# A top-k attention followed by a mixture of experts: the last batch's scores are computed at the start and kept in DRAM

## Chip, cores, metric

One core of a Trainium2 chip. The metric is the device time of one execution in microseconds; lower is better. Three runs of the kernel before gave 1983.19, 1984.89 and 1987.19 us, median 1984.89.

## What is computed

```python
def _attn_ref(q, k, v):                    # (4 batches, 8 heads, 576 rows, 64)
    scores = scale * np.matmul(q, k.transpose(0, 1, 3, 2))
    kth = np.partition(scores, -32, axis=-1)[..., -32:-31]
    scores = np.where(scores >= kth, scores, -1e9)
    attn = softmax(scores)
    return attn @ v
def _moe_ref(x, w_gate, w1, w2):           # x: (2304, 512), 8 experts, hidden 1024
    P = exp(x @ w_gate - max);  P = 8 rounds of row and column normalisation
    for e in range(8):
        out += P[:, e:e+1] * (np.maximum(x @ w1[e], 0) @ w2[e])
```

The attention output, its heads side by side, is the x of the second part. All experts see all rows.

## The kernel before

**Numbers.** All is float32. TensorE is fed with pairs: a rounded high part made by ScalarE (`hi_act`, line 75) and the rest, made by a subtraction on GpSimd (`lo_pool`, L81) or on VectorE (`lo_dve`, L84). A product of two such operands is three matmuls, or two in the scores, where q holds its high part in partitions 0 to 63 and its low part in 64 to 127.

**Attention** runs in seven stages (`STAGES`, L25), in this order: batch 0 rows 0 to 255, batch 0 rows 256 to 511, the same two of batch 1, both of batch 2, the last 64 rows of batch 0 (`attend_rest`), and both of batch 3. Each stage walks four pairs of heads. For a pair `attend_heads` loads q, k and v, splits them, and `attend_phase` takes two tiles of 128 rows for each of the two heads: `scores` (L116, L117) makes a 128x576 tile in the one PSUM tile `sp`, with four matmuls of 288 columns; `copy_scores` (L125, L123) brings it to an SBUF tile `s` on ScalarE; `topk` runs four MAX8 and three MATCH_REPLACE8 on VectorE and masks the exponentials (`Et`, L145); `normalise` scales; TensorE transposes (L233), the result is split again and multiplied with v (L246, L247). The last 64 rows of two heads go through `rest_weights` as one more tile of scores (12 matmuls, 2304 columns).

**Experts.** Rows are grouped in blocks of 256. Blocks 0 to 4 take turns on two seats (`BOARD`, L32): block i boards at turn 4i and stays for 8 turns, one expert each (`visit`). A visit loads w1 and w2 (tile `wr`, L395), splits them (`wh` on ScalarE, `wl` on GpSimd), makes the hidden layer (L413, stored by L462 and L463) and the output (L500), which goes to DRAM through tile `y` (L508, L510). For block 0, half of the hidden layer (the first 256 of 512 inputs) is made early by `first_half` for all eight experts, 32 PSUM tiles of it: weights in `wr` (L432), matmuls L443, copy to `y` L446, store to DRAM L448. The first turns read it back with L452 and need only the other half. When attention has ended, `sinkhorn` makes P, `right_factors` (L563 and the lines around it) prepares blocks 5 to 8, which are then multiplied in a seven-product scheme (L611) with the output part L670, while the stored outputs are read back (L524) and summed.

**What sets the order.** The program is written as one stream; a planner orders it for each engine when the kernel is built, by priority (attention first, by `high_priority`), then by the place in the program, and each engine runs its list strictly in order. Tiles of one name share a fixed number of buffers: `wr` 3, `wh` and `wl` 6 each, `y` 4, PSUM `p2` 2, `p1` 2, `s` 3, `raw` 3, `kh` and `kl` 2 each. `first_half` and all visits use `wr` and `y`. All DMAs of the lines named here are issued from the SP queue.

Of the kernel before, what the change touches and what calls it, by code (L numbers as in the profile page):

```python
# [36 lines left out]
LAST = [5, 6, 7, 8]  # L37
OFF = {(0, 0): 3}
# [5 lines left out]
def kernel(  # L44
# [74 lines left out]

    def copy_scores(sp):  # L120
# [45 lines left out]
    def attend_heads(b, hp, phases, xts, xm):  # L166
# [13 lines left out]
        if phases:  # L180
            qs = load_phase(phases[0])
        ks = []
        for i in range(2):
# [18 lines left out]
        for ph in phases:  # L202
            if ph != phases[0]:
                qs = load_phase(ph)
            last = ph == phases[-1] and xm is not None
            qm = load_q("qm", 1024, 256, 1) if last else None
            attend_phase(hp, qs, qm, ks, xts[ph], xm if last else None, OFF.get((b, ph), 0))
# [3 lines left out]
    def attend_phase(hp, qs, qm, ks, xt, xm, off):  # L211
# [3 lines left out]
        for t in range(2):  # L215
# [3 lines left out]
            for i in range(2):  # L219
                o = i * 256 + t * 128  # L220
                qc = qs[:, o:o + 128]
                sp = scores([((a, 0, 288), [(qc, ks[i], slice(a * 288, a * 288 + 288))]) for a in range(2)])
                units.append((copy_scores(sp[:, :, 0:288]), Et[:, i, :], st[:, 0, i:i + 1]))
# [12 lines left out]
        if xm is not None:  # L236
            def put(rows, blocks, src):
                evac(ath[rows, blocks, 256:320], atl[rows, blocks, 256:320], src)
            rest_weights(qm, ks, put)
# [16 lines left out]
    def rest_weights(qm, ks, put):  # L256
        Et = ap_.tile([128, 2, S], F32, name="Et", bufs=2)
        st = ap_.tile([128, 2, 2], F32, name="st", bufs=3)
        qa, qb = qm[:, 0:128], qm[:, 128:256]
        sp = scores([  # L260
            ((0, 0, 256), [(qa, ks[0], slice(0, 256)), (qb, ks[1], slice(64, 320))]),
            ((0, 256, 512), [(qa, ks[0], slice(256, 512)), (qb, ks[1], slice(320, 576))]),
            ((1, 0, 64), [(qa, ks[0], slice(512, 576)), (qb, ks[1], slice(0, 64))]),
        ])
        topk([(copy_scores(sp.rearrange("p a b -> p (a b)")[:, 0:S]), Et[:, 0, :], st[:, 0, 0:1])])
# [12 lines left out]
    def attend_rest(b, hp, qm, ks, xm):  # L278
# [7 lines left out]
        rest_weights(qm, ks, put)  # L286
# [408 lines left out]
    x2 = psx = None  # L695
    stages_until(-1)
# [71 lines left out]
```

## Time and profile before

| | |
|---|---|
| median of 3 runs | 1984.89 us (1983.19 to 1987.19) |
| the profiled execution: time, span | 1985.03 us, 1982.8 us |
| mean granted TensorE clock | 0.987 of full |
| TensorE busy (matmul) | 1886.4 us, 95% |
| VectorE, GpSimd, ScalarE busy | 1478.0, 1100.1, 1045.3 us |
| DMA | 238.97 MB, mean 121 GB/s |

The time exceeds the span by 2.2 us of start and end. Matmuls overlap each other, so a matmul's duration is longer than what it costs TensorE; the distance from one start to the next is what it costs. Instructions of VectorE, ScalarE and GpSimd stand one behind the other, with an overlap of less than 0.15 us.

### The profile page before, as it was taken

Reading aid. Unit: us, or ns where it says so; the run is one execution under the profiler, and the core shown is the slowest. Engines: PE = TensorE matmul, PEld = TensorE weight load, DVE = VectorE, ACT = ScalarE, POOL = GpSimd, SP = SyncE. Lnnn points to the kernel's source line nnn. Section 1 sums busy time; section 2 is a strip of 40 time slices with the busy share of each in tenths; the row PEclk is TensorE's granted clock in tenths of the full one; section 3 lists DMA queues with packets and bytes.
Section 4 is the critical chain, followed back from the end, with each engine's and each line's share of the span. In section 5 each row is a group of like instructions: output and inputs, shape, how many; then the busy total and the mean of one; then the engine's idle time right before and its main releaser. Section 6 shows DMA issues by size and latency. Waiting matters only on the chain.

```text
span 1982.8 us, 27234 instructions
## 1 busy us (share of the span) xinstructions
PE 1886.4 (95%) x9571; PEld 1581.2 (80%) x9571; DVE 1478.0 (75%) x2828; ACT 1045.3 (53%) x1715; POOL 1100.1 (55%) x978
## 2 busy tenths in 40 slices
PE   4798889999999999999999999899999999999998
PEld 3677778988887888888888888778888888888887
DVE  9999999999998999962999996335555555543333
ACT  5766657666666666655665666443333333333331
POOL 4557876665564455455554457895454554545440
PEclk9899989999999999999999999999999999999999
DMA  3477554444343333234433325333333333311111
GB/s 114 129 241 240 179 189 143 153 136 140 122 128 121 108 111 122 90 127 139 132 122 100 103 94 176 123 121 122 101 101 111 116 105 109 102 55 57 56 42 43
DMA packets 95785, 238.97 MB, mean 121 GB/s; under 512 B 10784, under 2 KB 12960, under 8 KB 95648
## 3 DMA queue, kind: packets, MB, share of 16 engines
q1 hardware_dynamic: 95648, 237.23, 37.3%
q8 instruction: 75, 1.23, 0.3%
q14 instruction: 62, 0.51, 0.1%
HBM read 203.11 MB, written 34.08 MB: 120 GB/s over the span
## 4 chain that ended last, share of the span: by engine, by line
PE 55%; DVE 34%; POOL 3%; DMA 3%; issue 2%; ACT 2%; SPq 0%; POOLq 0%; ACTq 0%; DVEq 0%
PE p L670 18%; DVE m L136 11%; DVE w L143 9%; PE p L611 9%; PE p L500 8%; PE p L413 8%; DVE Et L145 5%; PE pc L611 4%; DVE hl L463 4%; DVE atl L84 3%; PE pb L611 2%; POOL wl L81 2%; DMA wr<-in_w_dram 1%; PE pt L233 1%; DMA raw<-in_q_dram 1%
## 5 line engine op out<-in xcount | busy, mean ns | idle before, releaser
L81 POOL TENSOR_TENSOR wl<-wr,wh 128x1024 fp32r<-128x1024 f32 x280 | 683.1, 2451 | 466.3 <-ACT wh L75 453.1
L75 ACT ACTIVATE wh<-wr 128x1024 fp32r<-128x1024 f32 x280 | 294.6, 1059 | 270.2 <-PE p L611 181.6
L136 DVE MAX8 m<-w 128x8 f32<-128x576 f32 x432 | 317.8, 748 | 1.7
L413 PE MATMUL p<-xh,wh 128*128 128x256 f32 (+1 forms) x768 | 266.6, 347 | 13.1 <-DVE y L458 7.3
L413 PE MATMUL p<-xh,wl 128*128 128x256 f32 (+1 forms) x768 | 264.3, 345 | 0.2 <-POOL wl L81 0.2
L413 PE MATMUL p<-xl,wh 128*128 128x256 f32 (+1 forms) x768 | 263.8, 344 | 0.0
L500 PE MATMUL p<-wh,hl 128*128 128x512 f32 x640 | 248.0, 398 | 4.5 <-DVE hl L463 4.5
L500 PE MATMUL p<-wh,hh 128*128 128x512 f32 x640 | 252.0, 397 | 0.3 <-ACT hh L462 0.3
L500 PE MATMUL p<-wl,hh 128*128 128x512 f32 x640 | 250.8, 395 | 0.2 <-POOL wl L81 0.2
L517 DVE SCALAR_TENSOR_TENSOR acc<-p,P,acc 128x512 f32<-128x512 f32 x120 | 89.5, 750 | 167.3 <-PE p L670 167.3
L143 DVE MATCH_REPLACE8 w<-m,w 128x576 f32<-128x576 f32 x288 | 213.2, 741 | 0.2
L670 PE MATMUL p<-wh,h2h 128*128 128x512 f32 x512 | 199.8, 391 | 1.3 <-ACT h2h L634 0.7
L670 PE MATMUL p<-wl,h2h 128*128 128x512 f32 x512 | 199.9, 390 | 0.0
L670 PE MATMUL p<-wh,h2l 128*128 128x512 f32 x512 | 196.7, 390 | 0.0
L413 PEld LDWEIGHTS p<-xh,wh 128*128 128x128 f32 x768 | 148.7, 194 | 34.1 <-DVE y L458 9.6
L145 DVE SCALAR_TENSOR_TENSOR Et<-s,m,Et 128x576 f32<-128x576 f32 x144 | 161.4, 1128 | 16.8 <-ACT Et L139 15.8
L413 PEld LDWEIGHTS p<-xh,wl 128*128 128x128 f32 x768 | 149.0, 194 | 14.6 <-issue 0.4
L413 PEld LDWEIGHTS p<-xl,wh 128*128 128x128 f32 x768 | 149.0, 194 | 14.5
L500 PEld LDWEIGHTS p<-wh,hl 128*128 128x128 f32 x640 | 120.4, 189 | 28.6 <-DVE hl L463 6.2
L500 PEld LDWEIGHTS p<-wl,hh 128*128 128x128 f32 x640 | 120.9, 189 | 23.6 <-POOL wl L81 0.6
L500 PEld LDWEIGHTS p<-wh,hh 128*128 128x128 f32 x640 | 121.0, 190 | 23.0 <-issue 1.3
L152 ACT ACTIVATE Et<-Et,st 128x576 f32<-128x576 f32 x144 | 104.9, 770 | 55.8 <-DVE st L150 55.6
(179 smaller groups left out, 4059.8 us busy)
## 6 DMA issues: line engine op xcount, KB each, us to landing
wr<-in_w_dram SPq DMA_DIRECT2D x240, 512.0 KB, 3.5
y<-y SPq DMA_DIRECT2D x160, 256.0 KB, 2.7
raw<-in_k_dram SPq DMA_DIRECT2D x56, 288.0 KB, 3.0
wr<-in_w_dram SPq DMA_DIRECT2D x48, 256.0 KB, 3.6
raw<-in_q_dram SPq DMA_DIRECT2D x32, 256.0 KB, 3.0
p<-y SPq DMA_DIRECT2D x32, 256.0 KB, 3.5
y<-p SPq DMA_DIRECT2D x32, 256.0 KB, 4.1
raw<-in_v_dram SPq DMA_DIRECT2D x28, 288.0 KB, 3.0
```

The source lines that it names most:

```text
L75: nc.scalar.activation(dst, src, AF.Copy)
L81: nc.gpsimd.tensor_tensor(dst, src, hi.bitcast(F32), op=OP.subtract)
L136: nc.vector.max(m8[u][:, r, :], ws[u] if r else s)
L143: nc.vector.match_replace(ws[u], m8[u][:, r, :], ws[u] if r else s, LOWEST)
L145: nc.vector.scalar_tensor_tensor(Em, s, m8[u][:, 3, 7:8], Em, op0=OP.is_ge, op1=OP.mult, accum_out=rsum)
L152: nc.scalar.activation(Et[:, i, :], Et[:, i, :], AF.Copy, scale=st[:, 1, i:i + 1])
L413: nc.tensor.matmul(ps[:, fo, :], a[:, kk, fs], x[:, k0 + kk, cs], start=(i == 0), stop=(i == 3 * nk - 1))
L463: nc.vector.scalar_tensor_tensor(seat.hl[:, ft, cs], src, 0.0, seat.hh[:, ft, cs].bitcast(F32), op0=OP.max, op1=OP.subtract)
L500: nc.tensor.matmul(ps, a[:, ft, ts], m[:, ft % 2, :], start=(i == 0), stop=(i == 3 * NFT - 1))
L517: return nc.vector.scalar_tensor_tensor(ACC[t], y, g, ACC[t], op0=OP.mult, op1=OP.add)
L611: nc.tensor.matmul(ps, w[:, kk, :], x[:, kk, :], start=(fresh and i == 0), stop=(i == 5), skip_group_check=True)
L670: nc.tensor.matmul(ps, a[:, ft, ts], m[:, ft, :], start=(i == 0), stop=(i == 11))
```

## The change

The scores of batch 3 are made by a new generator, `scores_ahead`. It is stepped eight times, ahead of everything else in the program and at ordinary priority (below attention, and ahead of `first_half` and the visits). A step takes one head: it loads and splits k and q in the tiles `wr`, `wh` and `wl`, and for each of four tiles of 128 rows makes the scores in two halves of 288 columns, in PSUM tile `p2`; each half is copied by ScalarE to a tile `y` and stored to DRAM. Every second step adds the tile of the last 64 rows. When batch 3 is attended, `load_scores` brings each tile from DRAM to an `s` buffer (for the second head: to a buffer of `kh` or `kl`), in place of loading and splitting q and k, of the matmuls and of the copy. The core of the diff:

```diff
+AHEAD = [3]
...
+    def keep(key, parts):
+        kept[key] = dram.tile([128, S], F32, name="s" + "_".join(map(str, key)))
+        c = 0
+        for groups in parts:
+            ps = ps2.tile([128, 512], F32, name="p2")
+            y = op_.tile([128, 512], F32, name="y", bufs=YB)
+            n = 0
+            for width, terms in groups:
+                for i, (qc, (kh, kl), cs) in enumerate(terms):
+                    nc.tensor.matmul(ps[:, n:n + width], qc, kh[:, cs], start=(i == 0), stop=False)
+                    nc.tensor.matmul(ps[:, n:n + width], qc, kl[:, cs], start=False, stop=(i == len(terms) - 1))
+                n += width
+            nc.scalar.activation(y[:, 0:n], ps[:, 0:n], AF.Copy)
+            nc.sync.dma_start(kept[key][:, c:c + n], y[:, 0:n])
+            c += n
+
+    def load_scores(*key):
+        name = "s" if key[-1] == 0 or len(key) == 2 else ("kh", "kl")[key[3]]
+        s = ap_.tile([128, S], F32, name=name, bufs=NS if name == "s" else 2)
+        nc.sync.dma_start(s, kept[key])
+        return s
+
+    def scores_ahead():
+        for b in AHEAD:
+            for hp in range(HP):
+                ks, qm = [], None
+                for i in range(2):
+                    kr = wp.tile([128, S], F32, name="wr", bufs=WR)
+                    nc.sync.dma_start(kr, k[b, 2 * hp + i])
+                    kh = wp.tile([128, S], F32R, name="wh", bufs=WB)
+                    kl = wp.tile([128, S], F32R, name="wl", bufs=WB)
+                    hi_act(kh, kr)
+                    lo_pool(kl, kr, kh)
+                    ks.append((kh, kl))
+                    m = 512 + (256 if i == 0 else 0)
+                    qr = wp.tile([128, m], F32, name="wr", bufs=WR)
+                    for ph in range(2):
+                        o = ph * 512 + i * 256
+                        nc.sync.dma_start(qr[:, ph * 256:ph * 256 + 256], q[b, hp, :, o:o + 256])
+                    if i == 0:
+                        nc.sync.dma_start(qr[:, 512:768], q[b, hp, :, 1024:1280])
+                    qs = wp.tile([128, m], F32R, name="wh", bufs=WB)
+                    hi_act(qs, qr)
+                    lo_pool(qs[64:128], qr[64:128], qs[64:128])
+                    if i == 0:
+                        qm = qs[:, 512:768]
+                    for ph in range(2):
+                        for t in range(2):
+                            qc = qs[:, ph * 256 + t * 128:ph * 256 + t * 128 + 128]
+                            keep((b, hp, ph, t, i), [[(288, [(qc, ks[i], slice(a * 288, a * 288 + 288))])]
+                                                     for a in range(2)])
+                    if i == 1:
+                        groups = [(d[2] - d[1], terms) for d, terms in rest_groups(qm[:, 0:128], qm[:, 128:256], ks)]
+                        keep((b, hp), [groups[0:2], groups[2:3]])
+                    yield
+
+    early = scores_ahead()
...
-        for i in range(2):
+        for i in range(0 if ahead else 2):
             kr = ap_.tile([128, S], F32, name="raw", bufs=RAW)
...
+                if b in AHEAD:
+                    s = load_scores(b, hp, ph, t, i)
+                else:
+                    o = i * 256 + t * 128
+                    qc = qs[:, o:o + 128]
+                    s = copy_scores(scores([((a, 0, 288), [(qc, ks[i], slice(a * 288, a * 288 + 288))])
+                                            for a in range(2)])[:, :, 0:288])
...
+        if b in AHEAD:
+            s = load_scores(b, hp)
+        else:
+            sp = scores(rest_groups(qm[:, 0:128], qm[:, 128:256], ks))
...
     x2 = psx = None
+    for _ in range(8):
+        next(early, None)
     stages_until(-1)
```

## Rows read from the trace of the kernel before

**Rows 1.** The page: busy time of each engine, and the span in 40 equal slices (a digit is TensorE's busy share in tenths).
```profile
PE 1886.4 (95%) x9571; PEld 1581.2 (80%) x9571; DVE 1478.0 (75%) x2828; ACT 1045.3 (53%) x1715; POOL 1100.1 (55%) x978
...
PE   4798889999999999999999999899999999999998
```

**Rows 2.** Busy time by stretch: start and end of the stretch, its length, then busy us (and instructions) of PE, PE's weight loads, DVE, ACT, POOL, then granted clock, DMA share, GB/s.
```profile
0.00:77.00 77.00, 35.78 (x144) 27.73 (x145) 72.31 (x153) 47.80 (x81) 40.38 (x68) 0.89 0.30 89
77.00:156.00 79.00, 75.53 (x394) 63.66 (x393) 72.89 (x157) 57.25 (x109) 39.00 (x55) 1.00 0.76 247
156.00:295.00 139.00, 114.17 (x648) 98.36 (x648) 137.61 (x233) 88.39 (x139) 107.73 (x91) 0.93 0.60 198
295.00:935.00 640.00, 631.00 (x3502) 538.11 (x3501) 572.60 (x1192) 403.83 (x691) 355.72 (x347) 1.00 0.39 126
935.00:1242.00 307.00, 303.73 (x1658) 259.64 (x1656) 285.50 (x590) 193.97 (x330) 166.88 (x156) 1.00 0.37 121
1242.00:1318.00 76.00, 67.35 (x376) 56.99 (x374) 23.92 (x77) 35.29 (x53) 70.43 (x49) 0.93 0.38 122
1318.00:1983.00 665.00, 658.80 (x2860) 536.66 (x2860) 313.15 (x430) 218.73 (x315) 319.97 (x215) 1.00 0.28 87
```

**Rows 3.** Groups of PE instructions, shapes apart, in the stretch of batch 3's attention (935 to 1242 us): count, then busy us and mean ns of one, then idle time before them. L117 has as many as L116 of each shape.
```profile
L116 PE MATMUL sp<-kh,qs 128*128 128x288 f32 x64 | 19.2, 309 | 0.0
...
L116 PE MATMUL sp<-kh,qm 128*128 128x256 f32 x16 | 4.2, 292 | 0.0
...
L116 PE MATMUL sp<-kh,qm 128*128 128x64 f32 x8 | 1.7, 235 | 0.0
```

**Rows 4.** PE's instructions in order of time: start us, duration us. Two pairs that follow each other without a break, one of 288 and one of 256 columns.
```profile
1185.62 0.29 PE L116 MATMUL sp<-kh,qs 128*128 128x288 f32 x1
1185.75 0.30 PE L117 MATMUL sp<-kl,qs 128*128 128x288 f32 x1
...
1199.52 0.28 PE L117 MATMUL sp<-kl,qm 128*128 128x256 f32 x1
1199.64 0.28 PE L116 MATMUL sp<-kh,qm 128*128 128x256 f32 x1
```

**Rows 5.** Single lines of the program: duration in ns as min/median/max, then the first and the last start in us; for a DMA the last row of each is the time from issue to landing. `first_half`'s copy and store, and the load that reads it back.
```profile
L446 ACT ACTIVATE y<-p x32: 572/592/620, 78.4 to 156.5; 128x512 f32<-128x512 f32 x32
...
L448 SPq DMA_DIRECT2D p<-y x32: 326/327/2362, 79.0 to 157.7; - x32
...
DMA to landing us min/median/max: 2.0/3.5/6.7
...
L452 SPq DMA_DIRECT2D y<-p x32: 319/380/1342, 155.7 to 449.2; - x32
```

**Rows 6.** Groups of ACT instructions in the whole span, shapes apart (columns as in Rows 3).
```profile
L75 ACT ACTIVATE kh<-raw 128x576 fp32r<-128x576 f32 x56 | 36.9, 680 | 13.3 <-PE sp L116 10.5 <-DMA raw<-in_k_dram 2.5
L75 ACT ACTIVATE qs<-raw 128x512 fp32r<-128x512 f32 x32 | 20.1, 629 | 27.4 <-DMA raw<-in_q_dram 27.4
L446 ACT ACTIVATE y<-p 128x512 f32<-128x512 f32 x32 | 18.9, 592 | 5.3 <-PE p L443 4.9 <-ACT lg L333 0.4
L160 ACT ACTIVATE tl<-pt 128x384 f32<-128x384 f32 x24 | 11.7, 485 | 4.5 <-POOL atl L81 2.7 <-PE pt L233 1.7
```

**Rows 7.** Groups of POOL instructions in the whole span.
```profile
L81 POOL TENSOR_TENSOR kl<-raw,kh 128x576 fp32r<-128x576 f32 x54 | 81.6, 1521 | 36.1 <-ACT kh L75 32.0 <-PE pt L233 3.9
L81 POOL TENSOR_TENSOR qs<-raw,qs 64x512 fp32r<-64x512 f32 x31 | 41.3, 1331 | 28.6 <-ACT qs L75 20.8 <-issue 3.5 <-PE pt L247 2.4
```

**Rows 8.** The masking instruction `Et` on VectorE from 0 to 100 us, and in the whole span (columns as in Rows 5).
```profile
L145 DVE SCALAR_TENSOR_TENSOR Et<-s,m,Et x14: 796/804/1511, 17.2 to 94.2; 128x576 f32<-128x576 f32 x14
...
L145 DVE SCALAR_TENSOR_TENSOR Et<-s,m,Et x144: 791/812/3017, 17.2 to 1222.5; 128x576 f32<-128x576 f32 x144
```

**Rows 9.** VectorE's instructions in order of time, between batch 0's last rows and batch 3: start us, duration, and in brackets the idle time before it and what ended it.
```profile
901.91 0.82 DVE L145 SCALAR_TENSOR_TENSOR Et<-s,m,Et 128x576 f32<-128x576 f32 x1 [15.43 <-ACT Et L139]
...
928.92 0.76 DVE L136 MAX8 m<-s 128x8 f32<-128x576 f32 x1 [5.99 <-ACT s L123]
```

**Rows 10.** Single lines again (columns as in Rows 5): the store of a visit's output and the load that brings it back at the end of the kernel.
```profile
L510 SPq DMA_DIRECT2D y<-y x80: 319/327/432, 187.1 to 1313.5; - x80
...
L524 SPq DMA_DIRECT2D y<-y x80: 319/320/694, 1312.5 to 1729.4; - x80
```

**Rows 11.** The chain that ended last, in the stretch 130 to 150 us: start us, us, what.
```profile
132.23 1.73 PE p L443 x8
```

**Rows 12.** Groups of PE instructions from 156 to 295 us (columns as in Rows 3): those of attention. L117 has as many as L116, L247 as many as L246.
```profile
L246 PE MATMUL pt<-ath,vz 128*128 128x256 f32 x40 | 10.3, 287 | 1.1 <-DVE atl L84 1.1
...
L233 PE MATMUL pt<-idt,Et 128*128 128x128 f32 x57 | 9.5, 290 | 1.2 <-DVE atl L84 0.7 <-ACT Et L152 0.5
L116 PE MATMUL sp<-kh,qs 128*128 128x288 f32 x28 | 9.3, 346 | 12.3 <-ACT s L125 12.3
```

**Rows 13.** SP's own waits from 0 to 160 us: who waited for whom, us in total, times, longest.
```profile
SPq L448 <- ACT y L446: 28.5, 19, 2.8
```

**Rows 14.** The chain that ended last, in the stretch 1195 to 1335 us: between the end of attention and the last part.
```profile
1244.65 1.82 PE pt L325 x8
...
1261.59 2.64 POOL tf L563 x3
...
1317.96 1.19 PE pc L611 x4
```

More of the change, by code (lines that the diff above doesn't have):

```diff
@@ L118, in scores, with rest_groups @@
         return sp
+    def rest_groups(qa, qb, ks):
+        return [
+            ((0, 0, 256), [(qa, ks[0], slice(0, 256)), (qb, ks[1], slice(64, 320))]),
+            ((0, 256, 512), [(qa, ks[0], slice(256, 512)), (qb, ks[1], slice(320, 576))]),
+            ((1, 0, 64), [(qa, ks[0], slice(512, 576)), (qb, ks[1], slice(0, 64))]),
+        ]
+    kept = {}
+    def keep(key, parts):
[13 more added lines that the diff above has]
+            c += n
@@ L178, in load_phase @@
             return load_q("qs", ph * 512, 512, 2)
-        if phases:
-            qs = load_phase(phases[0])
+        ahead = b in AHEAD
+        qs = load_phase(phases[0]) if phases and not ahead else None
         ks = []
-        for i in range(2):
+        for i in range(0 if ahead else 2):
             kr = ap_.tile([128, S], F32, name="raw", bufs=RAW)
@@ L202, in attend_heads, with attend_phase @@
         for ph in phases:
-            if ph != phases[0]:
+            if ph != phases[0] and not ahead:
                 qs = load_phase(ph)
             last = ph == phases[-1] and xm is not None
-            qm = load_q("qm", 1024, 256, 1) if last else None
-            attend_phase(hp, qs, qm, ks, xts[ph], xm if last else None, OFF.get((b, ph), 0))
+            qm = load_q("qm", 1024, 256, 1) if last and not ahead else None
+            attend_phase(b, hp, ph, qs, qm, ks, xts[ph], xm if last else None, OFF.get((b, ph), 0))
         if not phases:
             attend_rest(b, hp, load_q("qm", 1024, 256, 1), ks, xm)
-    def attend_phase(hp, qs, qm, ks, xt, xm, off):
+    def attend_phase(b, hp, ph, qs, qm, ks, xt, xm, off):
         nq = 256 if xm is None else 320
@@ L219, in attend_phase @@
             for i in range(2):
[L220 to L223, printed above, removed]
+                if b in AHEAD:
[5 more added lines that the diff above has]
+                                            for a in range(2)])[:, :, 0:288])
+                units.append((s, Et[:, i, :], st[:, 0, i:i + 1]))
             topk(units)
@@ L238, in put @@
                 evac(ath[rows, blocks, 256:320], atl[rows, blocks, 256:320], src)
-            rest_weights(qm, ks, put)
+            rest_weights(b, hp, qm, ks, put)
         tmp = ap_.tile([128, 320], F32, name="tmp", bufs=1)
@@ L252, in attend_phase, with rest_weights @@
                 nc.vector.tensor_tensor(xm[r, hp, :], av[r, 256:320], tmp[r, 256:320], op=OP.add)
-    def rest_weights(qm, ks, put):
+    def rest_weights(b, hp, qm, ks, put):
         Et = ap_.tile([128, 2, S], F32, name="Et", bufs=2)
         st = ap_.tile([128, 2, 2], F32, name="st", bufs=3)
[L259 to L265, printed above, removed]
+        if b in AHEAD:
+            s = load_scores(b, hp)
+        else:
+            sp = scores(rest_groups(qm[:, 0:128], qm[:, 128:256], ks))
+            s = copy_scores(sp.rearrange("p a b -> p (a b)")[:, 0:S])
+        topk([(s, Et[:, 0, :], st[:, 0, 0:1])])
         normalise(Et, st, 1)
@@ L284, in put @@
             nc.scalar.activation(at[rows, blocks, :], src, AF.Copy)
-        rest_weights(qm, ks, put)
+        rest_weights(b, hp, qm, ks, put)
         av = pst.tile([128, 512], F32, name="pt")
```

## The prediction

> **What bounds the kernel now.** I read the page first: TensorE is busy 95% of the span, and in the 40 slices it falls short only in the first ones [rows 1]. Then I cut the span by stages [rows 2]. From 295 us to the end PE is short of full by 9.0, 3.3, 8.7 and 6.2 us in stretches of 640, 307, 76 and 665 us: it is the bound there. Before that it is short by 41.2 us up to 77 us, by 3.5 us up to 156 us, and by 24.8 us up to 295 us. VectorE is nearly full to 295 us as well, with attention; it is the bound of the first 77 us, where PE has nothing but attention's matmuls.
>
> So matmuls taken out of the stretch behind 295 us shorten the kernel one for one, as long as what they cost at the start is free. That is the whole question.
>
> **What is removed behind 295 us.** Batch 3's scores are 64 matmuls of 288 columns on L116 and as many on L117, 16 and 16 of 256, and 8 and 8 of 64 [rows 3]. Their mean durations (309 ns) can't be added, since matmuls overlap; from start to start it is 0.13 us for 288 columns and 0.12 us for 256 [rows 4]. That makes 128 x 0.13 + 32 x 0.12 + 16 x 0.12 at most = 22.3 us. The ends are 20.5 us (the short ones free) and 25 us (0.1 us more for some 25 of the changes between scores and other work). I take 23 us. The 36 copies on ScalarE, the splitting of k and q on GpSimd and ScalarE, and 20 loads also leave this stage; PE is full beside them, so I count nothing. VectorE keeps all its work, 285.5 of 307 us in that stage [rows 2]. The 36 loads that come in are 288 KB each and can run ahead by the buffers of `s`, `kh` and `kl`; against some 8 us of VectorE for a tile (307 us for 36) stand 3.5 us from issue to landing, as for the 256 KB stores of `first_half` [rows 5], so they are covered. If the cover failed, VectorE would wait and PE would go on with visits.
>
> **What the same work costs at the start.** On PE 23 us, against 41.2 us of idle time up to 77 us: it fits. The engine that is short is ScalarE. For each of the eight heads it has one split of k (680 ns for 576 columns), one of q (629 ns for 512; with the 256 columns of the last rows about 840 ns), and eight copies of 288 columns. No row has that size; 384 columns took 485 and 512 took 592 ns [rows 6], so about 405 ns. Four last-row tiles add 592 and about 220 ns each. The sum of durations is 64 x 0.405 + 8 x 0.68 + 4 x 0.63 + 4 x 0.84 + 4 x 0.59 + 4 x 0.22 = 40.5 us; with 0.1 us of overlap for each of the 88 it is 32 us. These are the two ends. Attention leaves ScalarE 77 - 47.8 = 29.2 us up to 77 us, of which some 5 us come before the first k and q can have landed: 24 us. From 77 to 156 us it is busy 57.25 us, 18.9 us of it the copies of `first_half`, so 38.4 us are attention's and 0.51 us of each us is free [rows 2, 6]. The early scores end at 77 + (32 - 24)/0.51 = 93 us, or at 77 + (40.5 - 24)/0.51 = 109 us. I take 100 us.
>
> GpSimd gets 8 x 1.52 us for k and for q 4 x 1.33 plus about 4 x 2.0 us, 25.5 us in all [rows 7], with 36.6 us free up to 77 us [rows 2]: later than ScalarE in no case. A GpSimd instruction and a masking instruction of VectorE disturb each other: `Et` takes 0.79 us at best and 3.02 us at worst, yet 0.80 us in the median of the first 100 us, where GpSimd is busy half of the time [rows 8]. A quarter more GpSimd time on 14 of them, at up to 0.7 us each, is 2 to 3 us of VectorE at the start; VectorE has slack later, 15.4 us and 6.0 us in single waits ahead of batch 3 [rows 9], so I count nothing.
>
> The Trainium skill, page SBUF — State Buffer, section "Who interferes with whom", says that a VectorE instruction with two SBUF inputs and a GpSimd instruction that reads SBUF take turns, the second blocked until the first ends. By that rule each of the 16 added subtractions could hold back one masking instruction for all of its length, 25 us at the start in the worst case against my 2 to 3 us. The trace agrees that they collide (3.02 against 0.79 us), and no row shows that all would.
>
> **What is pushed back.** `first_half` needs buffers of `wr` and `y`, the same names that the early scores use, and the trace shows that buffers of one name are handed out in the order of the program. The load that reads a first half back could have gone soon after the first store had landed, at about 82 us; four buffers of `y`, each held some 4 us by a copy and a store, were not all in use by 32 copies in 78 us; still it was issued at 155.7 us, between the last but one copy and the last [rows 5]. At the end of the kernel it is the same: outputs stored since 187 us are loaded from 1312.5 us on, with the last spill store [rows 10]. So `first_half`, written behind the early scores, gets its first `y` only when they have had all their 72. It starts copying at 100 us and not at 78.4 us; one PSUM tile of eight matmul records, 1.73 us [rows 11], can be ready ahead. The delay is 20 us, between 13 and 29 us for the two ends.
>
> From 77 to 156 us PE is full with `first_half` [rows 2], so that work can't be made up, and the visits that follow in the same buffers come later by as much. They have 24.8 us of idle PE time up to 295 us, but those are waits inside the visits and behind attention, and GpSimd is busy 107.7 of 139 us there: I let nothing be made up, and take a gain of some us as the lower end. What is not lost is attention's share of PE, which goes on meanwhile: 80 matmuls at 0.12, 57 transposes at 0.1 and 56 scores at 0.13 us [rows 12] make 23 of 139 us, 17%. The delay costs 0.83 x 20 = 16.6 us.
>
> **The sum.** 23 - 16.6 = 6.4 us gained. The profiled execution took 1985.0 us, equal to the median within 0.2 us: 1978.5 us. By the ends of ScalarE's bound alone it runs from 23 - 11 = 12 us gained to 23 - 24 = 1 us lost, 1973 to 1986.
>
> **Rivals.**
>
> *All of it fits.* If the early scores end by 80 us, or `first_half` shares the buffers after all, nothing is pushed back and 23 us are gained: 1962 us. For it: 41.2 us of idle PE, and attention's own ScalarE work may give way a little. Against: the order of the buffers [rows 5, 10], and ScalarE's 24 free us for 32.
>
> *The SP queue holds the early scores up: slower.* All 72 stores go through SP, which runs in order, and each waits there for its copy. `first_half`'s 32 stores cost SP 28.5 us of waiting [rows 13], 0.9 us each, and 0.33 us to issue. At that price the 72 stores and 28 loads take SP 72 x 1.22 + 28 x 0.33 = 97 us, beside attention's own loads, which stand behind these waits and are needed on time. From about 8 us on that is an end at 105 us at best; with attention's loads and with ScalarE's attention work delayed, 125 us. Then the delay is 45 us, of which 37 are lost: 1985 + 14 = 1999 us. It turns into a loss from an end later than 108 us on. Against: the waits may be short where ScalarE has nothing else to do.
>
> *The end of attention holds the gain.* If visits end 23 us earlier but attention still ends at 1242 us, the factors are made from 1262 us on and the last part is packed only from 1318 us [rows 14]; PE would run dry ahead of it. GpSimd's work for visits would leave that stretch too (70.4 of 76 us busy [rows 2]), so perhaps 10 us stay: 1975 us.
>
> That the change doesn't do what it says (the planner moves the early scores behind `first_half`) is the first rival turned round: no idle time used, no gain, 1985 us. I see little room for it, as they come first in the program.
>
> **How the numbers follow.** The forecast has 0.42, of which 0.27 lie beyond 4 us of gain. All fits: 0.19. SP: 0.26. The end of attention: 0.11. Not moved: 0.02. A change within 0.2% (4 us) is about what a measurement of this kernel can't tell from none. Faster: 0.27 + 0.19 + 0.11 = 0.57. Same: 0.12 of the forecast, 0.03 of SP, 0.02: 0.17. Slower: 0.23 of SP and 0.03 of the forecast: 0.26. The range runs from 1961 us (all fits, 24 us) to 1998 us; it leaves out the worse half of the SP case and a gain greater than PE's price. The likeliest case alone is 1973 to 1986 us.
>
> **What would show it.** Batch 3's L116 and L117 gone from PE behind 900 us, and PE's idle time up to 77 us down by some 20 us. The last early copy at about 100 us, `first_half`'s first copy right behind it and its last at about 176 us in place of 156.5 us; the first visit's load of `y` at about 175 us. ScalarE near full up to then. The last part packed from about 1312 us. I am wrong if `first_half` starts at 80 us beside early scores (then it is the first rival), if the last early copy comes later than 110 us (the SP case, with SP's waits on ScalarE above 60 us), or if PE stands idle for more than 10 us between 1240 and 1320 us.

## The result: 1999.7 us, slower by 0.6%

The changed kernel took 1999.66 us (median of 4 runs, 1996.35 to 2000.17) against 1984.83 us: a ratio of 1.0061 with a 95% interval of 1.0048 to 1.0073. I had predicted 1978.5 us, 1961 to 1998, and faster. The profiled execution took 1996.35 us with a span of 1994.1 us.

The page (busy times, then TensorE by slices), for [rows 1]:

```profile
PE 1896.5 (95%) x9571; PEld 1589.9 (80%) x9571; DVE 1481.0 (74%) x2828; ACT 1044.4 (52%) x1747; POOL 1097.2 (55%) x974
...
PE   6799888999999999999999999969999999999998
```

Stretches as in [rows 2]:

```profile
0.00:77.00 77.00, 49.84 (x220) 39.75 (x221) 67.78 (x136) 59.70 (x125) 51.51 (x65) 0.91 0.75 229
77.00:156.00 79.00, 71.62 (x384) 63.43 (x383) 69.17 (x150) 63.03 (x128) 44.09 (x69) 0.91 0.70 228
156.00:295.00 139.00, 121.46 (x684) 104.38 (x683) 132.24 (x231) 91.81 (x149) 104.38 (x86) 0.94 0.68 221
...
935.00:1242.00 307.00, 302.71 (x1587) 254.37 (x1586) 281.83 (x585) 174.01 (x285) 163.06 (x147) 1.00 0.48 156
1242.00:1318.00 76.00, 64.69 (x400) 55.43 (x398) 26.87 (x78) 38.08 (x64) 63.55 (x46) 0.94 0.40 132
```

TensorE has 14.1 us more work up to 77 us (I had said some 20). VectorE, the bound there, has 4.5 us less in the first stretch, 3.7 less in the second and 5.4 less in the third: attention falls behind. The early copy, `first_half`'s copy and the load that reads it back, for [rows 5]:

```profile
L145 ACT ACTIVATE y<-p x72: 218/410/655, 17.5 to 102.5; 128x288 f32<-128x288 f32 x64, 128x512 f32<-128x512 f32 x4, 128x64 f32<-128x64 f32 x4
...
L521 ACT ACTIVATE y<-p x32: 569/592/617, 104.3 to 180.2; 128x512 f32<-128x512 f32 x32
...
L527 SPq DMA_DIRECT2D y<-p x32: 319/374/490, 180.5 to 471.0; - x32
```

The last early copy starts at 102.5 us (predicted 100), `first_half`'s first right behind it and its last at 180.2 us (predicted 176), and the first visit's load comes at 180.5 us (175). SP's wait, for [rows 13]:

```profile
SPq L146 <- ACT y L145: 36.9, 38, 3.4
```

That is short of the 60 us that would have meant the SP case. Now the two ends: the last store of a visit's output [rows 10], and VectorE's `xt`, the finished output of attention (two for each pair of heads in a stage), whose last is the end of attention (changed kernel, then the kernel before):

```profile
L585 SPq DMA_DIRECT2D y<-y x80: 319/327/1180, 213.5 to 1302.9; - x80
...
L326 DVE TENSOR_TENSOR xt<-pt,tmp x64: 393/422/430, 69.1 to 1269.9; 64x256 f32<-64x256 f32 x64
```

```profile
L250 DVE TENSOR_TENSOR xt<-pt,tmp x64: 394/423/431, 48.9 to 1241.1; 64x256 f32<-64x256 f32 x64
```

The visits end 10.6 us earlier (1313.5 to 1302.9), attention 28.8 us later. What follows waits for attention (chain that ended last, for [rows 14]):

```profile
1288.65 2.69 POOL tf L638 x3
...
1310.39 2.30 POOL wl L83
...
1319.38 2.08 PE p L686 x4
...
1334.75 0.46 PE p L745 x2
```

The factors start at 1288.65 us and not 1261.59, and TensorE has little to do until they are there: from 1300 to 1345 us it is busy 28.9 us, in the kernel before 43.7. Between 1240 and 1320 us it is idle for 12.7 us (8.7 before): of my three signs of being wrong, this one came.

### The profile page after: what moved, and what is told of

Read it like the earlier page. It is cut to its first block, busy times and chain, and to the rows that moved or that the text cites. A ratio compares the mean times of both kernels' runs of the same rounds, so it can differ in the third digit from the quotient of the medians.

```text
span 1994.1 us, 27526 instructions
## 1 busy us (share of the span) xinstructions
PE 1896.5 (95%) x9571; PEld 1589.9 (80%) x9571; DVE 1481.0 (74%) x2828; ACT 1044.4 (52%) x1747; POOL 1097.2 (55%) x974
## 4 chain that ended last, share of the span: by engine, by line
PE 56%; DVE 30%; DMA 5%; POOL 4%; issue 2%; ACT 2%; SPq 0%; POOLq 0%; ACTq 0%; DVEq 0%
PE p L745 18%; DVE m L208 10%; PE p L686 9%; PE p L575 8%; PE p L488 8%; DVE w L215 8%; DVE Et L217 5%; PE pc L686 5%; DVE hl L538 3%; DVE atl L86 2%; PE pb L686 2%; PE p L518 1%; POOL wl L83 1%; PE pt L309 1%; DMA raw<-in_q_dram 1%
## 5 line engine op out<-in xcount | busy, mean ns | idle before, releaser
L83 POOL TENSOR_TENSOR wl<-wr,wh 128x1024 fp32r<-128x1024 f32 (+1 forms) x288 | 696.4, 2428 | 478.4 <-ACT wh L77 470.1
L77 ACT ACTIVATE wh<-wr 128x1024 fp32r<-128x1024 f32 (+3 forms) x296 | 306.7, 1040 | 291.0 <-PE p L686 193.8
L488 PEld LDWEIGHTS p<-xh,wh 128*128 128x128 f32 x768 | 148.3, 193 | 39.0 <-DVE y L533 11.7
L217 DVE SCALAR_TENSOR_TENSOR Et<-s,m,Et 128x576 f32<-128x576 f32 x128 | 150.7, 1183 | 14.0 <-ACT Et L211 13.4
L575 PEld LDWEIGHTS p<-wh,hl 128*128 128x128 f32 x640 | 120.6, 189 | 27.9 <-DVE hl L538 5.2
L575 PEld LDWEIGHTS p<-wh,hh 128*128 128x128 f32 x640 | 121.4, 190 | 23.6 <-ACT hh L537 1.6
```

Source lines behind the costliest of these rows:

```text
L77: nc.scalar.activation(dst, src, AF.Copy)
L83: nc.gpsimd.tensor_tensor(dst, src, hi.bitcast(F32), op=OP.subtract)
L217: nc.vector.scalar_tensor_tensor(Em, s, m8[u][:, 3, 7:8], Em, op0=OP.is_ge, op1=OP.mult, accum_out=rsum)
L488: nc.tensor.matmul(ps[:, fo, :], a[:, kk, fs], x[:, k0 + kk, cs], start=(i == 0), stop=(i == 3 * nk - 1))
L575: nc.tensor.matmul(ps, a[:, ft, ts], m[:, ft % 2, :], start=(i == 0), stop=(i == 3 * NFT - 1))
```

## The experiments

Below, V is the start of the last output's first store (two stores of 128 rows each; the second is the last in the row shown) and A the start of the last `xt`. "Input" is the start of the `xt` that completes the input of `first_half`: the last one of the second pair of heads, in e8 and e12 of the third. These and the span are of the profiled execution, whose time lies up to 8 us from the median. The runs shared their chip time with runs of the kernel before (1987 to 1989 us there); ratios are against those. From e10 on, all runs but e13 load batch 3's tiles from the input k, as e1 does.

| run | us | ratio (95%) | input | `first_half` copies from | batch 2 attended | A | V | span |
|---|---|---|---|---|---|---|---|---|
| before | 1984.83 | 1 | 75.9 | 78.4 | 877.9 | 1241.1 | 1312.1 | 1982.8 |
| changed | 1999.66 | 1.0061 (1.0048 to 1.0073) | 101.9 | 104.3 | 899.9 | 1269.9 | 1302.0 | 1994.1 |
| e1_loads_only | 1976.98 | 0.9941 (0.9923 to 0.9959) | 77.4 | 79.9 | 880.4 | 1259.1 | 1284.0 | 1978.2 |
| e2_early_only | 2019.85 | 1.0156 (1.0138 to 1.0174) | 102.1 | 104.6 | 896.4 | 1263.2 | 1344.6 | 2014.5 |
| e3_own_buffers | 2012.96 | 1.0133 (1.0115 to 1.0150) | 96.0 | 100.2 | 906.4 | 1279.3 | 1323.3 | 2012.1 |
| e9_after_wb5 | 2001.46 (one run) | - | 98.2 | 111.5 | 897.0 | 1276.6 | 1308.0 | 1999.7 |
| e4_rest_interleaved | 1996.88 | 1.0035 (1.0018 to 1.0052) | 102.2 | 104.6 | - | 1232.5 | 1324.3 | 1995.1 |
| e5_before_interleaved | 1982.59 | 0.9977 (0.9966 to 0.9989) | 76.5 | 79.0 | - | 1192.5 | 1310.4 | 1980.3 |
| e6_half | 1987.34 | 1.0005 (0.9993 to 1.0016) | 88.3 | 92.2 | 880.8 | 1244.7 | 1312.5 | 1983.5 |
| e8_push_only | 1996.56 | 1.0049 (1.0034 to 1.0064) | 101.5 | 106.3 | 867.0 | 1232.7 | 1328.0 | 1996.2 |
| e10_matmuls_only | 1993.74 | 1.0035 (1.0021 to 1.0049) | 88.6 | 93.7 | 898.7 | 1272.5 | 1297.0 | 1993.1 |
| e11_no_stores | 1998.95 | 1.0057 (1.0040 to 1.0075) | 97.3 | 102.2 | 896.5 | 1272.2 | 1305.2 | 1996.2 |
| e12_loads_push | 1978.57 | 0.9949 (0.9926 to 0.9972) | 101.0 | 105.7 | 868.2 | 1236.7 | 1305.5 | 1976.7 |
| e13_two_interleaved | 1992.99 | 1.0021 (1.0006 to 1.0036) | 102.8 | 105.3 | - | 1233.6 | 1314.5 | 1983.4 |
| e14_splits_only | 1992.16 | 1.0027 (1.0011 to 1.0042) | 88.8 | 93.9 | 890.6 | 1264.2 | 1297.2 | 1987.6 |
| e15_one_split | 1988.06 | 1.0006 (0.9996 to 1.0016) | 77.4 | 79.9 | 874.6 | 1244.2 | 1315.0 | 1986.1 |
| e16_one_split_wb6 | 1977.14 | 0.9940 (0.9924 to 0.9957) | 77.6 | 80.2 | 883.1 | 1259.5 | 1284.8 | 1979.1 |

**Two ends.** Span minus V is 668 to 672 us in before, e2, e4, e5, e6, e8, e12, e13 and e15; span minus A is 719 to 724 us in the others but e3 (733 us). But for e3, the span is the greater of V + 670 and A + 722 us within some 4 us. Before: 1982 and 1963, so visits bounded it, with 19 us to spare for attention. Changed: 1972 and 1992. This sum was found in the runs, not predicted.

**e1: the loads alone.** No early work; batch 3's tiles are loaded from the input k.

```diff
-    for _ in range(8):
-        next(early, None)
...
-        nc.sync.dma_start(s, kept[key])
+        nc.sync.dma_start(s, k[key[0], 2 * key[1] + (key[4] if len(key) > 2 else 0)])
```

> Leaves out the early scores altogether; batch 3 attends over tiles of the same size loaded from the input k, so this is the change's end without its start. Theory A (the last part waits for the end of batch 3's attention, which the work at the start has made late; the visits no longer count): nothing is late at the start, attention ends at 1235 to 1241 us as before, the visits end near 1289 us (1312 less 23), TensorE idles some 10 us ahead of the last part: 1968 to 1978 us. Theory B (first_half and with it the visits and the boarding of block 4 are pushed, and that alone delays batch 3): the same, nothing is pushed here. Theory C (batch 3's attention itself is slower because its tiles come from DRAM through the SP queue): the attention of batch 3, 301 us before and 319 us after the change, stays above 312 us, ends behind 1250 us, and the time is 1985 us or more.

V comes 28.1 us earlier. Up to V, TensorE is busy for 1199.5 us in place of 1223.0, which is 23.5 us less, and idle for 4.6 us less. The time falls only 11.7 us, for A is now the later end; it is 18 us later than before, with no early work at all.

**e2: the early work alone.** Batch 3 is attended as before.

```diff
-        ahead = b in AHEAD
+        ahead = False
...
-                if b in AHEAD:
+                if False:
```

> Early scores made and stored, but batch 3 attended as in the kernel before: the change's start without its end. Theories A and B: attention is some 22 us late when batch 2 ends (878 us before) as in the changed kernel, TensorE has its 23 us of matmuls behind 900 us again, so the visits end near 1335 us and the time is 2005 to 2012 us. If the removed matmuls are worth nothing in the changed kernel because attention's end rules anyway (A in its strict form), the time is that of the changed kernel, 1997 to 2002 us. Theory C: 1985 to 1995 us, the loads were the loss.

Some 19 us slower than the whole change by the ratios; here V is the end that counts.

**e3: buffers of its own for the early scores** (and `wh`, `wl` with 5 buffers, for room, as in e9, the changed kernel with that alone). The q of the last rows is split in a tile of its own, and their scores are copied in three parts.

```diff
-        y = op_.tile([128, 512], F32, name="y", bufs=YB)
+        y = op_.tile([128, 288], F32, name="ya", bufs=3)
...
-                    kr = wp.tile([128, S], F32, name="wr", bufs=WR)
+                    kr = wp.tile([128, S], F32, name="wa", bufs=2)
```

> The changed kernel with buffers of its own for the early scores' raw k and q and for their copies, so that first_half no longer queues behind them; the room comes from wh and wl, 5 buffers each in place of 6 (e9 is the changed kernel with that alone). Theory A (attention, slowed at the start by the early work, rules the end: time = end of attention + 722 us, as 724 and 719 us in the changed kernel and in e1): first_half starts near 80 us, the visits come 10 to 25 us earlier, but ScalarE is as loaded, attention stays some 18 us late at 156 us and ends at 1260 to 1272 us: 1985 to 1996 us, at most 10 us better than e9. Theory B (the push of first_half is the loss): the visits are back and the time falls to 1968 to 1980 us.

In e9 `first_half` has its input at 98.2 us and its matmuls run from 100.1 us, yet it copies only from 111.5 us, behind the last early copy at 111.2: there the hand-out order did hold it. In e3 it copies 11 us sooner, 4 us behind its input, among early copies that go on to 130.4 us. That is not the 80 us I expected, for the input itself is late. Nothing is won: attention and visits are both later. Why V came so late here stays open.

**e4 and e5: batch 0's last rows pair by pair behind batch 3's pairs**, in the changed kernel and in the one before.

```diff
-STAGES = [... (2, (0, 1), 1), (0, (), 1), (3, (0, 1), 1)]
+STAGES = [... (2, (0, 1), 1), (3, (0, 1), 1)]
...
             attend_heads(b, hp, phases, xts, xm)
+            if b == 3:
+                attend_heads(0, hp, (), {}, X["m", 0, 1][:, :, 0:64])
```

> The changed kernel with one more edit: the four pairs of batch 0's last rows, a stage of its own between batch 2 and batch 3 in which VectorE is half idle, are attended one by one behind the four pairs of batch 3. Nothing changes at the start. Theory A: batch 3 starts some 40 us earlier, attention ends at 1225 to 1240 us in place of 1270 us, the last part starts when the visits end (1302 us): 1973 to 1985 us. Theory B: first_half, visits and the boarding of block 4 (965 us) are as late as before, so batch 3 can't come earlier and the time stays at 1995 to 2000 us.

> The kernel before with the same edit as e4 (batch 0's last rows between the pairs of batch 3). Theory A: attention ends near 1205 us, but the visits end at 1312 us as before and TensorE is full up to then, so only the short idle times ahead of the last part go: 1977 to 1985 us. If attention's end ruled before the change too, the time falls by 20 us or more, under 1965 us.

A falls by 37.4 and 48.6 us. I read it so: the waits of VectorE in that stage [rows 9] are a chain of four pairs, one after the other, and other work fills them only if it is written there. In e4 V rises by 22.3 us in return and the time is not won; e5 is the one version with the whole computation that beats both kernels.

**e6: half of the heads ahead** (pairs 0 and 1 of batch 3).

> Only the first two of batch 3's four pairs of heads are made ahead; the others as in the kernel before. Theory A: the early work ends near 60 us, so first_half is not pushed (first copy by 82 us), and attention is late by half as much, 8 to 10 us: it ends at 1250 to 1257 us, and 722 us more make 1972 to 1979 us; TensorE's own sum, with 11.5 us fewer matmuls at the end of the visits, would allow 1971 us. Theory B: with no push there is no loss: 1968 to 1975 us. If both are wrong and the loads at the end are the loss: 1985 us or more.

Neither gain nor loss: V as before, A 3.6 us later. VectorE runs four MAX8 for each tile of 128 rows, 576 in all, and their count shows how far attention is. The start is as late as with the whole early work (the 96th MAX8 ends at 178.7 us, before at 160.5), but 4.0 us are left of that at the 320th, at 661 us.

**e8: the push alone.** The kernel before, `first_half` over inputs 128 to 383, which exist one pair later.

```diff
-            if (b, phases, hp) == (0, (0,), 2):
+            if (b, phases, hp) == (0, (0,), 3):
...
-                            ... x[:, kk, :],
+                            ... x[:, 1 + kk, :],
```

(The second half takes the other inputs, 0 to 127 and 384 to 511.)

> The kernel before, with first_half over inputs 128 to 383 in place of 0 to 255 (the second half takes the rest): it needs the third pair of heads and can start only near 106 us in place of 78 us, with no early scores. This prices the push alone. My prediction's step (0.83 of the delay is lost, nothing made up): the visits end near 1335 us, 2005 to 2009 us. Theory A on attention: it is at most 5 us late at 156 us and ends before 1250 us, so what is lost is lost by the visits. If the push is made up by idle time (24.8 us up to 295 us): 1985 to 1993 us.

The start is 27.9 us later, V 15.9 us; attention is even 8.4 us *earlier*. A late `first_half` is not what delays attention.

**e12: what the prediction counted, together.** e1 with e8's edit: matmuls removed, `first_half` pushed, no early work.

> The loads-only run (no early work, batch 3 attends tiles loaded from the input k) with first_half taking inputs 128 to 383, which are there one pair of heads later, so that it starts at about 106 us as in the changed kernel. Leaves out the values of batch 3's scores. It holds all that the prediction counted: 23 us of matmuls removed, first_half pushed back, and VectorE's delay at the start counted as nothing. If the delay of attention by the early work is the failed step: the last visit store is at 1284 + 16 = 1300 us, attention ends near 1251 us (the push alone brought it 8 us forward), and the time is the greater of 1300 + 672 and 1251 + 724: 1970 to 1980 us. If the push and the loads together are enough to bring the loss: attention ends at 1265 us or later and the time is 1990 us or more.

It took 1978.57 us. Its `first_half` copy, `xt` and last store:

```profile
L521 ACT ACTIVATE y<-p x32: 569/597/629, 105.7 to 180.9; 128x512 f32<-128x512 f32 x32
...
L326 DVE TENSOR_TENSOR xt<-pt,tmp x64: 393/422/431, 49.3 to 1236.7; 64x256 f32<-64x256 f32 x64
...
L585 SPq DMA_DIRECT2D y<-y x80: 319/327/796, 210.2 to 1306.9; - x80
```

The push is the changed kernel's; attention ends 33 us sooner and the last store comes 4 us later. So the loss against the forecast is the early work's own hold on attention.

**e10 and e11: how much of the early work.** In e10 the PSUM tiles are neither copied nor stored, in e11 copied but not stored.

```diff
-            nc.scalar.activation(y[:, 0:n], ps[:, 0:n], AF.Copy)
-            nc.sync.dma_start(kept[key][:, c:c + n], y[:, 0:n])
```

> The early matmuls, with the loads and splits of k and q, but their PSUM tiles are neither copied nor stored; batch 3 attends tiles loaded from the input k in place of scores, as in the loads-only run. Leaves out the values of batch 3's scores. The loads-only run, without any early work, took 1977 us: its first_half copied from 79.9 us on, its attention ended at 1259.1 us, its last visit store was at 1284.0 us. Theory C (ScalarE, with 72 copies more in its list, is what makes attention and first_half late): here ScalarE has only 16 splits, some 10 us, more; first_half starts at 82 to 90 us, batch 2's attention ends within 6 us of 880 us, attention ends at 1257 to 1264 us: 1976 to 1984 us. Theory P (attention's matmuls wait behind the early ones in PE's list): batch 2's attention ends as late as in the changed kernel, near 900 us, attention ends at 1270 us: 1990 to 1996 us.

> As the run with early matmuls alone, and their PSUM tiles are copied to y by ScalarE, but not stored; y comes free at the end of the copy. Leaves out the values of batch 3's scores. Theory C (the copies on ScalarE): the last early copy still comes at 97 to 103 us, first_half follows at 99 to 106 us, batch 2's attention ends at 893 to 900 us, attention at 1264 to 1272 us: 1987 to 1996 us. Theory S (SP's 72 stores with their waits, and y held by them): the copies end by 90 us, batch 2's attention within 6 us of 880 us: 1976 to 1984 us.

My theory C (the 72 copies) falls: without copies and stores attention ends as late. The stores cost nothing that shows in the time (1998.95 against 1999.66 us); the copies bring `first_half` from 93.7 to 102.2 us and some 5 us of time.

**e14, e15, e16: matmuls or splits.** e14 has the early loads and splits without matmuls. e15 and e16 have all the matmuls from one k and one q, split once; e15 with 5 buffers of `wh` and `wl`, e16 with 6.

```diff
-                nc.tensor.matmul(ps[:, n:n + width], qc, kh[:, cs], start=(i == 0), stop=False)
...
-                    nc.sync.dma_start(kr, k[b, 2 * hp + i])
...
+        nc.sync.dma_start(kr, k[3, 0])
...
+        ks = [(kh, kl), (kh, kl)]
```

(The first line removed is e14's, the others e15's and e16's.)

> Of the early work only the loads and the splits of k and q on ScalarE and GpSimd; no early matmul, copy or store. Batch 3 attends tiles loaded from the input k. Leaves out the values of batch 3's scores. With the early matmuls as well the run took 1993.74 us, its 96th MAX8 ended at 171.3 us, its first_half copied from 93.7 us on, batch 2's attention ended at 898.7 us and batch 3's at 1272.5 us; with no early work and the same push of first_half 154.7, 105.7, 868.2 and 1236.7 us. Theory P (the early matmuls in TensorE's ordered list, which wait there for their operands, take attention's slack): without them the 96th MAX8 ends by 163 us, batch 2's attention by 884 us, batch 3's by 1262 us: 1974 to 1984 us. Theory G (the splits, 11 us on ScalarE and 25 us on GpSimd, are enough): the 96th MAX8 at 168 us or later, batch 2's attention at 892 us or later, 1989 us or more.

> The early matmuls in full number (160 for the full tiles and the last rows), all from one k and one q that are loaded and split once; PSUM neither copied nor stored; wh and wl have 5 buffers in place of 6, which cost the changed kernel 2 us. Batch 3 attends tiles loaded from the input k. Leaves out the values of batch 3's scores. The operands are there from about 15 us on, so no early matmul waits for a split. Theory P1 (the length of the matmuls alone, in TensorE's list): the 96th MAX8 at 168 us or later, attention's end at 1268 us or later, 1990 to 1997 us. Theory P2 (not their length but their waits for operands that GpSimd and ScalarE make): attention's first tiles come up to 10 us later while the early matmuls run, then nothing more: the 96th MAX8 by 163 us, attention's end by 1262 us, 1974 to 1984 us.

> As the run with all early matmuls from one k and one q, split once, but wh and wl have their 6 buffers again (the early operands take two of wh and one of wl until the last early matmul). PSUM neither copied nor stored; batch 3 attends tiles loaded from the input k. Leaves out the values of batch 3's scores. With 5 buffers first_half copied from 79.9 us and the 96th MAX8 came at 160.7 us, as without early work, yet the last visit store came at 1315.0 us and the time was 1988.06 us; the loads-only run has 1284.0 us and 1976.98 us. If the early matmuls are free (the fifth buffer alone was the loss): last visit store at 1284 to 1294 us, attention's end at 1255 to 1264 us, 1975 to 1984 us. If the matmuls cost something later than the first 160 us: last visit store at 1305 us or later, 1986 us or more.

The same three lines, e14, then e16:

```profile
L511 ACT ACTIVATE y<-p x32: 575/593/631, 93.9 to 169.5; 128x512 f32<-128x512 f32 x32
...
L316 DVE TENSOR_TENSOR xt<-pt,tmp x64: 396/422/430, 63.1 to 1264.2; 64x256 f32<-64x256 f32 x64
...
L575 SPq DMA_DIRECT2D y<-y x80: 319/327/474, 198.4 to 1298.1; - x80
```

```profile
L510 ACT ACTIVATE y<-p x32: 573/592/616, 80.2 to 157.3; 128x512 f32<-128x512 f32 x32
...
L315 DVE TENSOR_TENSOR xt<-pt,tmp x64: 394/422/431, 50.4 to 1259.5; 64x256 f32<-64x256 f32 x64
...
L574 SPq DMA_DIRECT2D y<-y x80: 319/327/913, 188.8 to 1287.5; - x80
```

e16 takes e1's time with all 23 us of matmuls added: they are free when their operands are there. e15 is 11 us above it, with one buffer less of `wh` and `wl` and names of their own for the early operands. e14, which has not one early matmul, loses 15.2 us against e1 by the medians (9.4 us between the two profiled executions). The splits and their loads are enough; these two, and the splits' shares on ScalarE and GpSimd, were not parted.

The input of `first_half` sums it up. Without early work it is complete at 77.4 us (e1), with the matmuls and a single split at 77.6 (e16), with the splits at 88.8 (e14), with splits and matmuls at 88.6 (e10), with the copies too at 97.3 (e11), and with the stores at 101.9 us (changed). And `first_half`'s first copy starts 2.4 to 5.1 us behind it in every run but e9. So the late start in the runs with early work is attention's own delay.

Where it begins is seen in `atl` on GpSimd, which TensorE needs for attention's product with v (up to 60 us; before, changed, e14, e16):

```profile
L81 POOL TENSOR_TENSOR atl<-tl,ath x9: 994/996/1607, 27.3 to 58.6; 128x384 fp32r<-128x384 f32 x9
```

```profile
L83 POOL TENSOR_TENSOR atl<-tl,ath x5: 989/997/1016, 39.9 to 57.6; 128x384 fp32r<-128x384 f32 x5
```

```profile
L83 POOL TENSOR_TENSOR atl<-tl,ath x5: 996/998/1002, 36.3 to 57.6; 128x384 fp32r<-128x384 f32 x5
```

```profile
L83 POOL TENSOR_TENSOR atl<-tl,ath x8: 997/1014/1602, 30.0 to 57.5; 128x384 fp32r<-128x384 f32 x8
```

With the splits the first comes 9 to 12.6 us later, and five are done in place of eight or nine. The 9 us of e14 can be followed. GpSimd in order of time:

```profile
24.03 2.31 POOL L83 TENSOR_TENSOR wh<-wr,wh 64x768 fp32r<-64x768 f32 x1
...
26.58 1.41 POOL L83 TENSOR_TENSOR wl<-wr,wh 128x576 fp32r<-128x576 f32 x1
28.06 1.26 POOL L83 TENSOR_TENSOR qs<-raw,qs 64x512 fp32r<-64x512 f32 x1
29.42 0.19 POOL L211 TENSOR_SCALAR st<-st 128x2 f32<-128x2 f32 x1
...
34.97 1.41 POOL L83 TENSOR_TENSOR wl<-wr,wh 128x576 fp32r<-128x576 f32 x1
36.33 1.00 POOL L83 TENSOR_TENSOR atl<-tl,ath 128x384 fp32r<-128x384 f32 x1
```

`st`, a sum of 0.19 us, has its operand from VectorE at 24.7 us. It starts at 29.42 us, behind two early splits (`wh`, `wl`) and a split of attention's q, and VectorE's next step on it is late:

```profile
24.59 0.08 DVE L207 DVE_READ_ACCUMULATOR Et<-s,m,Et 128x1 f32 x1
...
29.64 0.17 DVE L212 RECIPROCAL st<-st 128x2 f32<-128x2 f32 x1 [0.81 <-POOL st L211]
```

In the kernel before the same `st` started 0.1 us after its operand, and `ath` followed `tl` on ScalarE at once (GpSimd, then ScalarE):

```profile
23.01 0.19 POOL L149 TENSOR_SCALAR st<-st 128x2 f32<-128x2 f32 x1 [1.84 <-DVE Et L145]
```

```profile
26.20 0.49 ACT L160 ACTIVATE tl<-pt 128x384 f32<-128x384 f32 x1 [0.33 <-PE pt L233]
26.72 0.53 ACT L75 ACTIVATE ath<-tl 128x384 fp32r<-128x384 f32 x1
```

In e14 an early split stands between them on ScalarE and waits there for its load:

```profile
32.52 0.48 ACT L222 ACTIVATE tl<-pt 128x384 f32<-128x384 f32 x1
34.02 0.68 ACT L77 ACTIVATE wh<-wr 128x576 fp32r<-128x576 f32 x1 [1.02 <-DMA wr<-in_k_dram]
34.61 0.51 ACT L77 ACTIVATE ath<-tl 128x384 fp32r<-128x384 f32 x1
```

So `st` is 6.4 us later than before, `ath` 7.9 and `atl`, behind one more early split, 9.0. This is the first pair of heads only. The last early split of e14 starts at 49.6 us on GpSimd; how its later delays come about was not followed.

**e13: two of the four pairs interleaved**, in the changed kernel.

> The changed kernel with two of the four pairs of batch 0's last rows attended behind batch 3's first two pairs, the others where they were. All four interleaved moved attention's end from 1269.9 to 1232.5 us and the last visit store from 1302.0 to 1324.3 us. Theory of two ends (the time is the greater of the last visit store + 672 and attention's end + 724): half of each is 1251 and 1313 us, so 1976 to 1986 us, about 10 us under the changed kernel and close to the kernel before. If the two ends don't add so: the changed kernel's time within 3 us.

It took 1992.99 us, more than the 1976 to 1986 us expected, though the profiled execution, its fastest, took 1985.3. There V is where half of the effect puts it (1314.5 us against 1313), but two pairs bring A as far forward as four (1233.6 and 1232.5 us). Why the median is 8 us above the profiled execution stays open.

## Why the prediction was wrong

**What bounds the kernel now**: right for visits. That attention is a second end, 19 us behind, was in the third rival only, and there as a limit to the gain, not as a way to a loss.

**What is removed**: 23 us was right; TensorE's busy time up to V falls by 23.5 us in e1. That the loads are covered held for their landing (VectorE waits 3.5 us in all for `s` from 960 us on). But batch 3 took longer: from batch 2's last `xt` to A it is 363.2 us before, 378.7 in e1 and 370.0 in the changed kernel. VectorE waits for ScalarE in that stretch (from 960 us on, `atl` for `ath` and `xt` for `tmp`: 9.1 us before, 19.0 in e1, 17.5 in the changed kernel). Why ScalarE is later was not tried.

**What the same work costs at the start**: TensorE, right (e16). ScalarE, right as far as the early copies go (102.5 against 100 us). **The step that failed is attention's delay at the start**: GpSimd "later than ScalarE in no case", VectorE's delay "2 to 3 us", and with its later slack "I count nothing". I compared GpSimd's 25.5 us with its 36.6 free us, as a sum, and asked only whether the early scores would be late. The question was what stands behind the early work in the lists of GpSimd and ScalarE, and that was attention's `st`, `ath` and `atl`. The second pair's output is 26.0 us late (101.9 against 75.9 us), and attention ends 28.8 us late. Of these, 22.0 us are there when batch 2 ends and 6.8 come in batch 3.

VectorE's own delay was not 2 to 3 us either: its 96th MAX8 ended at 160.5 us before, at 154.7 in e12, 170.5 in e14 and 178.4 in the changed kernel. Only 1.0 us of it are longer masking instructions (the 22 that end by then take 20.9 us before, 21.9 changed), so they stayed at my small price. The worst case that I worked out from the page SBUF — State Buffer of the Trainium skill ("Who interferes with whom"), an estimate of 25 us, didn't come. Most of the rest is idle time: 25.1 us up to the 96th MAX8 in place of 11.3, of which waits for ScalarE are 20.2 us (7.5 before) and for GpSimd 2.4 (2.1).

This delay isn't carried on unchanged. Against the kernel before, the changed kernel is 17.8 us late at the 96th MAX8, 5.5 at the 112th (220 us) and 22.3 at the 256th (545 us). Against e12, which has the same push, it is 23.6, 36.4 and 30.9 us late, and 34.7 at the last. Why the delay of half of the early work is made up by 661 us (e6) and that of the whole is not stays open.

**The slack of [rows 9]** was to take the delay in. It didn't: the changed kernel is 19.3 us late at the last MAX8 of batch 2 and 20.3 us at the last of the stage behind it. The same place in the changed kernel:

```profile
922.40 0.82 DVE L217 SCALAR_TENSOR_TENSOR Et<-s,m,Et 128x576 f32<-128x576 f32 x1 [8.09 <-ACT Et L211]
...
931.55 0.69 DVE L538 SCALAR_TENSOR_TENSOR hl<-p,hh 128x512 fp32r<-128x512 f32 x1 [7.84 <-ACT hh L537]
...
951.90 0.76 DVE L208 MAX8 m<-s 128x8 f32<-128x576 f32 x1 [4.03 <-ACT s L195]
```

VectorE waits in the stage of batch 0's last rows as it did (from 860 to 960 us it is busy 48.0 us, before 49.9). A wait inside a chain that starts later also starts later; here it gave back nothing.

**What is pushed back**: the number was right, 25.9 us of delay against 20 (13 to 29), but by luck. I had `first_half` wait for `y`, behind all 72 early copies. In the changed kernel the input came at the same time, and its matmuls ran only behind that (VectorE and TensorE, then the same in the kernel before):

```profile
101.41 0.88 DVE L326 TENSOR_TENSOR xt<-pt,tmp 64x256 f32<-64x256 f32 x2 [0.89 <-ACT tmp L325]
```

```profile
102.85 2.76 PE L518 MATMUL p<-xt,wr 128*128 128x256 f32 x12
```

```profile
75.89 0.43 DVE L250 TENSOR_TENSOR xt<-pt,tmp 64x256 f32<-64x256 f32 x1
```

```profile
76.76 2.76 PE L443 MATMUL p<-xt,wr 128*128 128x256 f32 x12
```

So without the wait for `y` it would have started as late. The buffers do hold it where the early copies end later than the input (e9). The price of the push came out as forecast: in e12 against e1 the start is 25.8 us later and V 21.5, which is 0.83. That it is the very figure is luck too, for in e8, where nothing is removed, 0.57 of the push was lost.

**The sum**, 6.4 us earlier, is what V did in e12: 1312.1 to 1305.5 us. The time there, 1978.57 us, is the forecast's number, but 9.3 us under the kernel before that ran beside it (1987.86 us). In the changed kernel V came 10.1 us earlier, and A decided: 28.8 us later, less the 19 us to spare, is 10 us; the span rose by 11.3.

**The rivals.** SP's 1999 us is the number that came, by coincidence: SP waited 36.9 us and the stores cost nothing that shows (e11). The end of attention holding the gain is e1 (1976.98 us against 1975), though attention ended there at 1259 us and not at 1242. All fits: e16 shows it for the matmuls, but V + 670 was then below A + 722.

## What to carry to other kernels

Work moved into an engine's free time costs what stands behind it in that engine's ordered list, so ask of each helper engine what comes next in its list and who waits for it; the sum of free time does not answer that. When a wait ends where you forecast it, look for a second wait that ends at the same time. Find the second end of the program (here attention) and how far it is behind the first before you count a delay of it at nothing. A wait inside a serial chain is no slack for what delays the chain's start.

## What the runs showed of the hardware

In e12 the mean granted clock of the first 77 us was 0.72, in the kernel before 0.89 (both between its two levels, 1.2 and 2.4 GHz), with TensorE busy 37.5 and 35.8 us; attention was no later for it (the 64th MAX8 ended at 102.9 and 102.8 us). At the other end a low clock cost time. In the changed kernel TensorE waits for the factors, and the stretch from 1309 to 1330 us, then the 9 us before it, read:

```profile
1309.00:1330.00 21.00, 9.04 (x25) 7.30 (x26) 11.21 (x42) 4.12 (x5) 19.83 (x15) 0.51 0.16 52
1300.00:1309.00 9.00, 4.90 (x23) 3.67 (x22) 4.83 (x19) 2.26 (x3) 9.00 (x10) 1.00 0.58 174
```

The granted clock is 0.51 over these 21 us, the lower level of 1.2 GHz, after 9 us in which TensorE was busy for 4.9, and it lasts into the first matmuls of the last part (1319.38 us): four of them take 2.08 us, in the kernel before 1.19 [rows 14]. A late factor was paid for twice, in idle time and in slower work behind it.
